# Two half pairs' weighted sums in one block every twelve steps, in an attention and expert kernel

## The chip, the core and the metric

One of the eight cores of a Trainium2 chip runs the kernel. The metric is the device time of one execution in microseconds (us). Engines: TensorE (PE; its weight loads are a queue of their own, PEld), VectorE (DVE), ScalarE (ACT), GpSimd (POOL) and SyncE (SP, which issues DMAs).

## The reference

Attention in which a query sees only the keys of its own hash bucket, and then a layer of eight experts with one expert per token:

```python
q_bits = (einsum('bhsd,dk->bhsk', q, proj) > 0)         # q, k, v: (4, 8, 768, 64); proj: (64, 6)
mask   = q_bucket[..., :, None] == k_bucket[..., None, :]
attn   = softmax(where(mask, scale * q @ k.T, -1e9))     # divided by (sum + 1e-9)
x      = (attn @ v).transpose(0, 2, 1, 3).reshape(3072, 512)
e_idx  = argmax(x @ w_gate)                              # 8 experts
out[t] = gate_w[t] * sigmoid(x[t] @ w_output_gate)[e] * (relu(x[t] @ w1[e]) @ w2[e])   # w1: 512x1024
```

## The kernel before

**The steps.** The 32 heads form 16 pairs. A pair has 2 heads x 6 query tiles of 128 rows, so 12 tiles, and the attention is a loop over 192 steps, one tile each. The order of instructions on PE, DVE, ACT and POOL is the order in which the code issues them; nothing reorders it. What one tile passes through:

- `scores`: four matmuls (L548) into `ps_s`, one of two PSUM buffers, then VectorE's eviction (L552), which clips, takes the row minimum and frees the buffer;
- `soft`: ScalarE's exponential in place (L560), which also sums each row;
- `normal`: for two tiles together, VectorE adds 1e-9 to the row sums and inverts them (L567, L568), and GpSimd scales the two tiles (L570);
- `transposed`: six TensorE transposes (L586) into the two buffers of `ps_t`, and two ScalarE copies from there into `pts` (L591);
- `weighted`: for a half pair (six tiles), 24 matmuls with the values into `ps_a` (L601), VectorE's copy into `ot` (L604), and in `rows` VectorE's transpose into `xb` (L613) and the DMA to `x_dram`.

Step s issues scores of tile s and, LAG = 6 steps behind, the transposes of tile s - 6. At every sixth step there is a **block** between these two: the weighted sums of one half pair, which need only data that is ready, and beneath them five exponentials on ScalarE (2 + 2 + 1). The sixth exponential of the six steps stands at the second step behind the block (k == 2), alone between the copies of two tiles. Two of the three pairs of tiles are scaled in the block, the third at k == 3.

**What else is hung into the steps.** `plan(step, fn)` puts work at the end of a step, `block(step, when, fn)` into a block at a named place. The projection of the next pair's queries and keys (`project`, 0.85 us of TensorE, and VectorE's sign bits, L417), the splitting of these into high and low parts (`split_hi` on GpSimd L495, `split_lo` on VectorE L502), and for each batch of four pairs the routing: `logits` and `tokens` (the experts' logits, transposed), `best` and `choose` (one-hot of the expert, ending in the cast L678 to `ohb`), `prefix` (matmuls of `ohb` with a triangle, L702, which give each token's place), `ranks`, `places` (L201 to L208), `gate_values` and `columns` (L689 to L218), `hot` (L223), and a table by matmuls (L229). Of the last batch but one, `pick` (L804 to L813) chooses an expert whose tokens and weights are then fetched and prepared (L178 to L181) while attention still runs.

Behind step 191 the remaining six tiles are transposed and copied alone (of the odd ones the transposes go to `ps_s`), then the expert stage follows, with the sums of the last half pair inside its first matmuls.

Of the kernel before, what the change touches and what calls it, by code (L numbers as in the profile page):

```python
# [59 lines left out]
def lsh_attention_then_moe(  # L60
# [61 lines left out]
    perm = cst.tile([P, E, E], F32, name="perm")  # L122
# [131 lines left out]
    def gather(idx, n=CH, ntok=NTOK, pool=gp, bufs=NCH):  # L254

        xg = pool.tile([CH, DM], F32, name="xg", bufs=bufs)
# [114 lines left out]
    with ExitStack() as actx:  # L371
# [14 lines left out]
        LAG = PER  # L386
# [153 lines left out]
        def scores(s):  # L540
# [10 lines left out]
            mn = sp.tile([P, 1], F32, name="mn", bufs=PER + 2)  # L551
# [20 lines left out]
        def transposed(s, pr):  # L572
# [6 lines left out]
            two = ps_s.tile([P, 2, 512], F32, name="ps_s") if last and s % 2 else None  # L579
            for h in range(2):  # L580
                if two is None:
                    tr = ps_t.tile([P, 3, P], F32, name="ps_t")
                else:
                    tr = two[:, h, 0:HS].rearrange("p (c q) -> p c q", c=3)
                for c in range(3):
                    nc.tensor.transpose(tr[:, c], pr[:, (3 * h + c) * P:(3 * h + c + 1) * P], ident)  # L586
                dst = pts[:, 3 * h:3 * h + 3, t * P:(t + 1) * P]
                if h and last:
                    nc.vector.tensor_copy(dst, tr)
                else:  # L590
                    nc.scalar.copy(dst, tr)  # L591

        def weighted(hb, c):
            g, hf = hb // 2, hb % 2
            st = pairs[g]
            if c == 0:
                st["av"] = ps_a.tile([P, HS], F32, name="ps_a")
            if c == NT - 1 and hf == 0:
                st["ot"] = gp.tile([P, S], F32, name="ot", bufs=4)
# [3 lines left out]
            if c == NT - 1:  # L603
                nc.vector.tensor_copy(st["ot"][:, hf * HS:(hf + 1) * HS], st["av"])  # L604
# [18 lines left out]
        def routing(b):  # L623
# [5 lines left out]
            def logits(hf, n):  # L629
                if hf == 0:  # L630
                    st["lt"] = gp.tile([P, S], F32, name="lt")
                pm = ps_m.tile([P, HS], F32, name="ps_m")
# [112 lines left out]
        for g in range(NP):  # L745
            s0 = 12 * (g - 1)
            if g >= 2:
                plan(max(s0 - 20, 8) if g > 2 else 2, lambda g=g: load(g))
                if g > 2:
                    block(s0 - PER, "matmuls", lambda g=g: project(g))  # L750
                else:
                    plan(8, lambda g=g: project(g))
                block(s0, "head", *(lambda g=g, j=j: split_hi(g, j) for j in range(2)))
                block(s0, "early", lambda g=g: split_lo(g, 0, 0))
                block(s0, "amid", lambda g=g: split_lo(g, 0, 1), lambda g=g: split_lo(g, 1, 0))
                block(s0, "behind", lambda g=g: split_lo(g, 1, 1), *(lambda g=g, j=j: spread(g, j) for j in range(2)))
            elif g == 1:
# [4 lines left out]
                for j in range(2):  # L762
                    for n in range(2):
                        plan(3 + n + (4 + n) * j, lambda j=j, n=n: split_lo(1, j, n))
                    plan(4 + 5 * j, lambda j=j: spread_lo(1, j), lambda j=j: spread_bits(1, j))
                plan(6, lambda: load_v(0))
            if g >= 1:
                plan(s0 + 10, lambda g=g: load_v(g))
            for hf in range(2 if g + 1 < NP else 1):
                block(12 * g + 6 * hf + 2 * PER, "matmuls", *(  # L770
                    lambda hb=2 * g + hf, c=c: weighted(hb, c) for c in range(NT)))
                if g + 1 < NP:
                    plan(12 * g + 6 * hf + 2 * PER, lambda g=g, hf=hf: rows(g, hf))
        for i, fn in enumerate(more_constants()):
            plan(18 + 2 * i, fn)
        for b in range(B - 1):
            r = routing(b)
            s0 = 12 * (H // 2) * (b + 1)
            for hf in range(2):
                block(s0 + PER * (hf + 1), "logits", lambda r=r, hf=hf: r["logits"](hf, H // 2))  # L780
            block(s0 + 3 * PER, "amid", r["choose"], r["gate_sums"])
            block(s0 + 5 * PER, "amid", r["gate_values"], r["columns"])
# [424 lines left out]
```

## Time and profile before

| | us |
|---|---|
| median of 3 runs (lowest, highest) | 760.28 (760.21, 760.89) |
| the profiled execution: its time, its span | 761.32, 759.6 |
| PE busy | 743.7 (98% of the span) |
| PEld busy | 606.1 (80%) |
| DVE busy | 489.6 (64%) |
| ACT busy | 459.9 (61%) |
| POOL busy | 377.2 (50%) |

The time of the profiled execution is longer than its span by 1.72 us, which lie around it. A share is an average over two stages: attention with routing up to about 440 us, the experts behind it. All rows of the trace below count from the start of the span.

### The profile page before, as it was taken

The page shows a single profiled execution, that of the slowest core. Times are in us where ns is not written, and L with a number is a line of the kernel's source. Part 1 is how long each engine was busy: PE and PEld are TensorE (multiplying, and loading weights), DVE is VectorE, ACT ScalarE, POOL GpSimd, SP SyncE. Part 2 cuts the span into 40 slices and gives each one's busy share as a digit, 9 for nine tenths or more (in the row PEclk, how much of TensorE's full clock was granted, in tenths as well). Part 3 has the DMA queues.
Part 4 walks back from the last instruction along what each step waited for, and adds up shares of the span by engine and source line. Part 5 has one row for each costly group of instructions (what it writes and reads, how often), then busy time and mean ns, then how long its engine had stood idle before and what let it go on. Part 6 is the DMA issues. An engine that isn't in the chain of part 4 may idle for free. (4 is left out here: it accounts for less than half of the span.)

```text
span 759.6 us, 13708 instructions
## 1 busy us (share of the span) xinstructions
PE 743.7 (98%) x4690; PEld 606.1 (80%) x4690; DVE 489.6 (64%) x1043; ACT 459.9 (61%) x930; POOL 377.2 (50%) x415
## 2 busy tenths in 40 slices
PE   7999999999999999999999999999999999999997
PEld 5776867677676777768687678888999999989895
DVE  7867776797776888667897684266353545454540
ACT  6778887877888787888888721253333344443331
POOL 6556553554555355454457923535446464645201
PEclk9999999999999999999999999999999999999999
DMA  6465555456565545555353422373434444536601
GB/s 208 117 151 133 121 134 124 109 126 136 128 124 125 127 106 130 131 133 120 77 118 108 122 59 84 103 270 118 131 128 152 160 151 155 184 123 223 203 12 40
DMA packets 84799, 98.89 MB, mean 130 GB/s; under 512 B 57999, under 2 KB 59439, under 8 KB 84720
## 3 DMA queue, kind: packets, MB, share of 16 engines
q1 hardware_dynamic: 79376, 84.58, 42.8%
q0 software_dynamic: 5200, 13.31, 5.4%
q8 instruction: 40, 0.66, 0.4%
q14 instruction: 39, 0.32, 0.1%
q10 hardware_dynamic: 144, 0.02, 0.0%
HBM read 59.49 MB, written 13.11 MB: 96 GB/s over the span
## 5 line engine op out<-in xcount | busy, mean ns | idle before, releaser
L570 POOL TENSOR_SCALAR sc<-sc,rsum 128x768 f32<-128x768 f32 x192 | 186.6, 985 | 188.4 <-DVE rsum L568 93.7
L552 DVE TENSOR_SCALAR_CACHE_REDUCE sc<-ps_s 128x768 f32<-128x768 f32 x192 | 182.4, 954 | 52.0 <-PE ps_s L548 47.8
L591 ACT COPY pts<-ps_t 128x384 f32<-128x384 f32 x375 | 161.4, 483 | 80.6 <-PE ps_t L586 79.8
L560 ACT ACTIVATE sc<-sc,mn 128x768 f32<-128x768 f32 x192 | 178.2, 935 | 4.0 <-DVE sc L552 4.0
L586 PE MATMUL ps_t<-ident,sc 128*128 128x128 f32 x1134 | 158.2, 275 | 0.0
L586 PEld LDWEIGHTS ps_t<-ident,sc 128*128 128x128 f32 x1134 | 132.0, 141 | 28.1 <-POOL sc L570 14.7
L601 PE MATMUL ps_a<-pts,vt 128*64 128x384 f32 x768 | 131.1, 490 | 0.0
L548 PE MATMUL ps_s<-xr,xl 128*128 128x384 f32 x384 | 114.7, 380 | 4.0 <-DVE sc L552 2.7
L601 PEld LDWEIGHTS ps_a<-pts,vt 128*64 128x64 f32 x768 | 52.2, 137 | 67.7 <-issue 67.5
L326 DVE SCALAR_TENSOR_TENSOR hl<-ps_s,hh 128x256 fp32r<-128x256 f32 (+8 forms) x40 | 34.0, 849 | 109.1 <-ACT hh L325 95.6
L548 PE MATMUL ps_s<-yr,yl 76*128 76x384 f32 x384 | 99.2, 339 | 1.0 <-POOL yr L455 1.0
L315 PE MATMUL ps_s<-xh,w1h 128*128 128x256 f32 (+7 forms) x288 | 97.0, 337 | 0.2 <-DVE hl L326 0.2
L315 PE MATMUL ps_s<-xh,w1l 128*128 128x256 f32 (+7 forms) x288 | 95.2, 331 | 0.3 <-DVE w1l L181 0.3
L315 PE MATMUL ps_s<-xlo,w1h 128*128 128x256 f32 (+7 forms) x288 | 95.3, 331 | 0.0
L289 POOL DMA_INDIRECT xq<-x_dram,idx x75 | 82.1, 1095 | 23.8 <-issue 20.8
L332 POOL DMA_INDIRECT out_dram<-yo,sid x29 | 30.9, 1067 | 120.6 <-ACT yo L331 76.4
L325 ACT ACTIVATE hh<-ps_s 128x256 fp32r<-128x256 f32 (+8 forms) x40 | 29.1, 727 | 101.5 <-PE ps_s L315 71.6
L548 PEld LDWEIGHTS ps_s<-yr,yl 76*128 76x128 f32 x384 | 70.1, 190 | 1.5 <-POOL yr L455 1.5
L548 PEld LDWEIGHTS ps_s<-xr,xl 128*128 128x128 f32 x384 | 58.3, 192 | 6.9 <-DVE sc L552 4.8
L315 PEld LDWEIGHTS ps_s<-xh,w1h 128*128 128x128 f32 x288 | 54.2, 188 | 2.5 <-DVE hl L326 0.7
L315 PEld LDWEIGHTS ps_s<-xh,w1l 128*128 128x128 f32 x288 | 54.1, 188 | 1.8 <-DVE w1l L181 0.7
L315 PEld LDWEIGHTS ps_s<-xlo,w1h 128*128 128x128 f32 x288 | 54.1, 188 | 1.3 <-DVE xlo L272 0.2
(211 smaller groups left out, 1021.1 us busy)
## 6 DMA issues: line engine op xcount, KB each, us to landing
w_raw<-in_w_dram SPq DMA_DIRECT2D x34, 512.0 KB
qk<-in_qkT_dram SPq DMA_DIRECT2D x32, 384.0 KB
xh<-in_w_dram SPq DMA_DIRECT2D x14, 512.0 KB
xlo<-in_w_dram SPq DMA_DIRECT2D x14, 512.0 KB
vt<-in_v_dram SPq DMA_DIRECT2D x16, 384.0 KB
xr<-xl SPq DMA_DIRECT2D x30, 192.0 KB
yr<-xl SPq DMA_DIRECT2D x30, 192.0 KB
xr<-yl SPq DMA_DIRECT2D x30, 192.0 KB
```

The source lines that it names most:

```text
L289: nc.gpsimd.indirect_dma_start(out=xq[:, k * P:(k + 1) * P], out_offset=None, in_=x_dram.rearrange("n (a f) -> (n a) f", a=NB32), in_offse ...
L315: nc.tensor.matmul(ps, l, r, start=first and k == 0, stop=last and k == len(pairs) - 1)
L325: nc.scalar.activation(hh, ph, AF.Relu)
L326: return lambda: nc.vector.scalar_tensor_tensor(hl, ph, 0.0, f32(hh), ALU.max, ALU.subtract)
L332: nc.gpsimd.indirect_dma_start(out=out[:, :], out_offset=bass.IndirectOffsetOnAxis(ap=sid[0:n, r, a:a + 1], axis=0), in_=yo[0:n], in_offse ...
L548: nc.tensor.matmul(ss[:, n, 0:HS], l[0:k, qs], r[0:k, n * HS:(n + 1) * HS], start=first, stop=not first)
L552: nc.vector.tensor_scalar(sc, ss[:, :, 0:HS], MASKED, None, ALU.min, ALU.min, accum_out=mn)
L560: nc.scalar.activation(pr, pr, AF.Exp, bias=mn, scale=-1.0, accum_out=sums[s // GROUP][:, k:k + 1])
L570: nc.gpsimd.tensor_scalar(live[s0 + k], live[s0 + k], rs[:, k:k + 1], 0.0, ALU.mult, ALU.add)
L586: nc.tensor.transpose(tr[:, c], pr[:, (3 * h + c) * P:(3 * h + c + 1) * P], ident)
L591: nc.scalar.copy(dst, tr)
L601: nc.tensor.matmul(st["av"][j * D:(j + 1) * D], st["v"][:, j, c], blocks[hb][j][:, c], start=(c == 0), stop=(c == NT - 1))
```

## The change

The block stands at every twelfth step, two steps later than before (SHIFT = 2: steps 14, 26, ... 194), and has the sums of two half pairs: the second half of one pair ("sums", into `ps_a`), then the first half of the next pair ("more", into `ps_m`). The transposes run LAG = 8 steps behind the scores (from step 14 on). Nine exponentials stand in the block (2 + 2 + 2 + 2 + 1), three alone at k = 2, 4 and 6. Four pairs of tiles are scaled in the block, the others at k = 3 and k = 7 (or k = 1). The copy of "more" out of `ps_m` ("done") stands behind routing work on VectorE. The logits go into `ps_t` and are copied by ScalarE behind the nine exponentials. `choose` moves out of a block to the end of a step with k = 7, one step ahead of `prefix`; `places` and `gate_values` with `columns` move into blocks. In the last six tiles, odd ones are copied by one ScalarE instruction. Two allocations move (`perm`, and the tiles of later gathers) and some loads, splits and weight preparations move by some steps.

```diff
-        LAG = PER
+        SHIFT = 2
+        LAG = PER + SHIFT
+        LONG = 2 * PER
...
-                dst = pts[:, 3 * h:3 * h + 3, t * P:(t + 1) * P]
-                if h and last:
-                    nc.vector.tensor_copy(dst, tr)
-                else:
-                    nc.scalar.copy(dst, tr)
+                    nc.tensor.transpose(trs[h][:, c], pr[:, (3 * h + c) * P:(3 * h + c + 1) * P], ident)
+                if two is None:
+                    (nc.vector.tensor_copy if h and last else nc.scalar.copy)(
+                        pts[:, 3 * h:3 * h + 3, t * P:(t + 1) * P], trs[h])
+            if two is not None:
+                nc.scalar.copy(pts.rearrange("p (h c) q -> p h c q", h=2)[:, :, :, t * P:(t + 1) * P],
+                               two[:, :, 0:HS].rearrange("p h (c q) -> p h c q", c=3))
...
-                st["av"] = ps_a.tile([P, HS], F32, name="ps_a")
+                st["av"] = (ps_a if hf else ps_m).tile([P, HS], F32, name="ps_a" if hf else "ps_m")
...
+        def weighed(hb):
+            g, hf = hb // 2, hb % 2
+            st = pairs[g]
+            if hf == 0:
+                st["ot"] = gp.tile([P, S], F32, name="ot", bufs=4)
+            nc.vector.tensor_copy(st["ot"][:, hf * HS:(hf + 1) * HS], st["av"])
...
-                pm = ps_m.tile([P, HS], F32, name="ps_m")
+                pm = ps_t.tile([P, HS], F32, name="ps_t")
...
+                at_block = LONG * ((hb + 3) // 2) + SHIFT
+                block(at_block, "sums" if hf else "more", *(lambda hb=hb, c=c: weighted(hb, c) for c in range(NT)))
+                block(at_block, "sums" if hf else "done", lambda hb=hb: weighed(hb))
+                if g + 1 < NP and hf:
+                    block(at_block, "routing", lambda g=g: rows(g, 1))
...
-            block(s0 + 3 * PER, "amid", r["choose"], r["gate_sums"])
-            block(s0 + 5 * PER, "amid", r["gate_values"], r["columns"])
...
+            block(s0 + LONG + SHIFT, "logits", *(lambda r=r, hf=hf: r["logits"](hf, H // 2) for hf in range(2)))
+            block(s0 + 2 * LONG + SHIFT, "routing", r["places"])
+            block(s0 + 3 * LONG + SHIFT, "routing", r["gate_values"], r["columns"])
+            for n, fn in ((15, lambda r=r: r["tokens"](0, H // 2)), (17, lambda r=r: r["tokens"](1, H // 2)),
+                          (19, r["best"]), (21, r["choose"]), (22, r["prefix"]), (23, r["gate_sums"]), (24, r["ranks"]),
+                          (42, r["hot"]), (44, r["table"]), (45, r["entries"])):
+                plan(s0 + n, fn)
...
-                    now("amid")
+                    now("project")
+                    normals()
                     softs(2)
+                    now("amid")
+                    normals()
+                    softs(2)
+                    now("behind")
                     normals()
-                    for when in ("logits", "matmuls", "behind"):
-                        now(when)
+                    softs(2)
+                    normals()
+                    now("sums")
+                    now("routing")
                     softs(1)
-                elif k == 3:
+                    for when in ("more", "logits", "done"):
+                        now(when)
+                elif k in (1, 3, 7):
                     normals()
-                if s >= LAG:
-                    transposed(s - LAG, live.pop(s - LAG))
-                if s >= PER and (k == 2 or s < 2 * PER and k in (1, 4)):
+                i = s - PER if s < LONG else s - LAG
+                if s >= PER and not LONG <= s < LONG + SHIFT:
+                    transposed(i, live.pop(i))
+                if s in (PER + 1, PER + 2, PER + 4) or s >= LONG + SHIFT and k in (2, 4, 6) or s >= NSTEP:
                     softs(1)
```

Line numbers of the changed kernel are a few higher from L548 on. Three places show how instructions stand. **ScalarE, two blocks of the second batch** (`L560`/`L561` is the exponential, `L591`/`L590` the copies of transposed tiles, x2 for the two halves of one). Before:

```order
L560 ACTIVATE sc,rsum<-sc,mn 128x768 x5
L591 COPY pts_2121<-ps_t 128x3x128 x2
L591 COPY pts_2122<-ps_t 128x3x128 x2
L591 COPY pts_2121<-ps_t 128x3x128 x2
L560 ACTIVATE sc,rsum<-sc,mn 128x768
L591 COPY pts_2122<-ps_t 128x3x128 x2
L591 COPY pts_2121<-ps_t 128x3x128 x2
L591 COPY pts_2122<-ps_t 128x3x128 x2
L560 ACTIVATE sc,rsum<-sc,mn 128x768 x5
```

The same engine in the changed kernel:

```order
L561 ACTIVATE sc,rsum<-sc,mn 128x768 x9
L590 COPY pts_2347<-ps_t 128x3x128 x2
L590 COPY pts_2348<-ps_t 128x3x128 x2
L590 COPY pts_2347<-ps_t 128x3x128 x2
L561 ACTIVATE sc,rsum<-sc,mn 128x768
L590 COPY pts_2348<-ps_t 128x3x128 x2
L590 COPY pts_2347<-ps_t 128x3x128 x2
L561 ACTIVATE sc,rsum<-sc,mn 128x768
L590 COPY pts_2348<-ps_t 128x3x128 x2
L590 COPY pts_2470<-ps_t 128x3x128 x2
L561 ACTIVATE sc,rsum<-sc,mn 128x768
```

Of twelve exponentials two stood alone between copies, now three do, with two tiles' copies between one and the next.

**VectorE at the choice of the expert** (`ohb` is what the prefix matmuls read; `sc,mn<-ps_s` is the eviction of scores). Before, in the block of step 66:

```order
L567 TENSOR_SCALAR rsum<-rsum 128x2
L568 RECIPROCAL rsum<-rsum 128x2
L671 TENSOR_SCALAR eq<-df 128x48
L672 TENSOR_TENSOR eq<-eq,expi 128x48
L674 TENSOR_REDUCE ei<-eq 128x6
L675 TENSOR_TENSOR oneh<-ei,expi 128x48
L678 CAST ohb<-oneh 128x48
L682 TENSOR_REDUCE den<-ex 128x6
L683 TENSOR_TENSOR en<-en,oneh 128x48
L685 TENSOR_REDUCE es<-en 128x6
```

Now at step 69, in the open steps, where TensorE has the scores and transposes of step 70 between this place and the prefix matmuls:

```order
L553 TENSOR_SCALAR sc,mn<-ps_s 128x768 x2
L568 TENSOR_SCALAR rsum<-rsum 128x2
L569 RECIPROCAL rsum<-rsum 128x2
L677 TENSOR_SCALAR eq<-df 128x48
L678 TENSOR_TENSOR eq<-eq,expi 128x48
L680 TENSOR_REDUCE ei<-eq 128x6
L681 TENSOR_TENSOR oneh<-ei,expi 128x48
L684 CAST ohb<-oneh 128x48
L553 TENSOR_SCALAR sc,mn<-ps_s 128x768 x2
```

The five instructions are the same; weighted sums ran beside them before, scores and transposes do now.

**VectorE at the gate values and columns** (`den` to `gate`, then `t_rhs`). Before, in the block of step 78, ahead of the second pair of row sums and of the copy out of `ps_a`:

```order
L567 TENSOR_SCALAR rsum<-rsum 128x2
L568 RECIPROCAL rsum<-rsum 128x2
L689 TENSOR_SCALAR den<-den 128x6
L690 TENSOR_SCALAR es<-es 128x6
L691 RECIPROCAL den<-den 128x6
L692 RECIPROCAL es<-es 128x6
L693 TENSOR_TENSOR gate<-den,es 128x6
L214 TENSOR_TENSOR t_rhs<-oneh,t_oa 128x192
L218 TENSOR_TENSOR t_rhs<-t_rhs,toki 128x192
L218 TENSOR_TENSOR t_rhs<-t_rhs,gate 128x192
L567 TENSOR_SCALAR rsum<-rsum 128x2
L568 RECIPROCAL rsum<-rsum 128x2
```

Now in the block of step 86, behind the fourth pair of row sums, the copy out of `ps_a` and its transpose:

```order
L619 STREAM_TRANSPOSE xb<-ot 128x384
L695 TENSOR_SCALAR den<-den 128x6
L696 TENSOR_SCALAR es<-es 128x6
L697 RECIPROCAL den<-den 128x6
L698 RECIPROCAL es<-es 128x6
L699 TENSOR_TENSOR gate<-den,es 128x6
L213 TENSOR_TENSOR t_rhs<-oneh,t_oa 128x192
L217 TENSOR_TENSOR t_rhs<-t_rhs,toki 128x192
L217 TENSOR_TENSOR t_rhs<-t_rhs,gate 128x192
L610 COPY ot<-ps_m 128x384
L553 TENSOR_SCALAR sc,mn<-ps_s 128x768 x3
```

The copy out of `ps_m` and the first eviction behind the block stand behind these eight instructions.

## Rows read from the trace of the kernel before

**Rows 1.** The profile page, the costliest groups of instructions over the whole program: line, engine, operation, out<-in, count | busy us, mean ns of one | idle time before them and what ended most of it.

```profile
L570 POOL TENSOR_SCALAR sc<-sc,rsum 128x768 f32<-128x768 f32 x192 | 186.6, 985 | 188.4 <-DVE rsum L568 93.7
```

**Rows 2.** Busy time of each engine in the stretch from the first weighted sum to the last transpose (us, then per engine busy time and count of instructions; the last three columns are the granted clock of TensorE as a share, the DMA share and GB/s).

```profile
29.60:441.50 411.90, 407.84 (x2843) 302.23 (x2842) 315.24 (x789) 328.06 (x749) 229.08 (x259) 1.00 0.54 124
```

**Rows 3.** The timeline of one block of before without routing work in it (start us, us, engine, line, operation, out<-in, count [idle before <-releaser]; a row of several instructions lasts from the first to the last of them): TensorE, then VectorE.

```profile
200.00 0.51 PE L548 MATMUL ps_s<-yr,yl 76*128 76x384 f32 x2
200.35 0.82 PE L586 MATMUL ps_t<-ident,sc 128*128 128x128 f32 x6
200.93 0.60 PE L548 MATMUL ps_s<-xr,xl 128*128 128x384 f32 x2
201.36 0.51 PE L548 MATMUL ps_s<-yr,yl 76*128 76x384 f32 x2
201.80 4.09 PE L601 MATMUL ps_a<-pts,vt 128*64 128x384 f32 x24
...
206.60 0.88 PE L586 MATMUL ps_t<-ident,sc 128*128 128x128 f32 x6
207.24 0.59 PE L548 MATMUL ps_s<-xr,xl 128*128 128x384 f32 x2
...
203.61 0.17 DVE L567 TENSOR_SCALAR rsum<-rsum 128x2 f32<-128x2 f32 x1 [0.64 <-ACT sc L560]
205.45 0.54 DVE L567 TENSOR_SCALAR rsum<-rsum 128x2 f32<-128x2 f32 x1 [1.47 <-ACT sc L560]
206.11 0.54 DVE L604 COPY ot<-ps_a 128x384 f32<-128x384 f32 x1
207.34 0.57 DVE L613 STREAM_TRANSPOSE xb<-ot 128x384 f32<-128x384 f32 x1
208.33 0.96 DVE L552 TENSOR_SCALAR_CACHE_REDUCE sc<-ps_s 128x768 f32<-128x768 f32 x1 [0.42 <-PE ps_s L548]
```

**Rows 4.** The timeline from the second to the fourth step behind that block, where one exponential stands between the copies of two tiles: ScalarE and TensorE, then the row sum that follows.

```profile
210.67 0.95 ACT L560 ACTIVATE sc<-sc,mn 128x768 f32<-128x768 f32 x1
211.76 0.51 PE L548 MATMUL ps_s<-yr,yl 76*128 76x384 f32 x2
212.22 0.85 PE L586 MATMUL ps_t<-ident,sc 128*128 128x128 f32 x6
212.82 0.60 PE L548 MATMUL ps_s<-xr,xl 128*128 128x384 f32 x2
...
211.93 0.16 DVE L567 TENSOR_SCALAR rsum<-rsum 128x2 f32<-128x2 f32 x1
```

**Rows 5.** The waits of TensorE's weight loads over the whole program (waiting engine and line <- what ended the wait: us in total, times, longest).

```profile
PEld ps_t L586 <- POOL sc L570: 14.7, 24, 0.6
PEld ps_t L586 <- issue: 7.4, 22, 0.6
```

**Rows 6.** The timeline around the block of step 66, whose second half pair of exponentials has the choice of the expert among them: VectorE's first and last instruction of the choice, then TensorE up to the prefix sums.

```profile
150.16 0.17 DVE L567 TENSOR_SCALAR rsum<-rsum 128x2 f32<-128x2 f32 x1 [0.65 <-ACT sc L560]
151.72 0.84 DVE L678 CAST ohb<-oneh 128x48 bf16<-128x48 f32 x1
...
153.16 0.88 PE L586 MATMUL ps_t<-ident,sc 128*128 128x128 f32 x6
154.38 0.18 PE L702 MATMUL ps_m<-ohb,tri 128*128 128x48 bf16 x1 [0.34 <-DVE bt L417]
```

**Rows 7.** The timeline of VectorE's routing work: the places of one batch (four steps after its prefix sums; the second row is the first instruction behind them), then the gate values and columns in the block of step 78 (first instruction, and the first one behind them).

```profile
160.87 0.32 DVE L201 TENSOR_TENSOR t_ge<-rank,chki 128x30 f32<-128x30 f32 x1
162.86 0.94 DVE L552 TENSOR_SCALAR_CACHE_REDUCE sc<-ps_s 128x768 f32<-128x768 f32 x1
...
177.00 0.15 DVE L689 TENSOR_SCALAR den<-den 128x6 f32<-128x6 f32 x1
179.63 0.15 DVE L567 TENSOR_SCALAR rsum<-rsum 128x2 f32<-128x2 f32 x1
```

**Rows 8.** The timeline of a late eviction behind the block of step 72 (the scores, the eviction of the step before, the weight loads that waited), and the first and last row of the pick of the leading expert (its first instruction, and the first one behind it).

```profile
167.44 0.52 PE L548 MATMUL ps_s<-yr,yl 76*128 76x384 f32 x2
168.95 0.92 DVE L552 TENSOR_SCALAR_CACHE_REDUCE sc<-ps_s 128x768 f32<-128x768 f32 x1
169.93 0.30 PEld L548 LDWEIGHTS ps_s<-xr,xl 128*128 128x128 f32 x2 [0.20 <-DVE sc L552]
...
384.25 0.16 DVE L804 SCALAR_TENSOR_TENSOR o_key<-base,expi 128x8 f32<-128x8 f32 x1
385.44 0.95 DVE L552 TENSOR_SCALAR_CACHE_REDUCE sc<-ps_s 128x768 f32<-128x768 f32 x1
```

**Rows 9.** The timeline of one GpSimd instruction of the expert stage's preparation (an expert's weights being split) and of ScalarE's copy of the logits out of PSUM.

```profile
430.14 2.37 POOL L181 TENSOR_TENSOR w1l<-w_raw,w1h 128x1024 fp32r<-128x1024 f32 x1
432.79 0.46 ACT L637 COPY lt<-ps_m 96x384 f32<-96x384 f32 x1
```

**Rows 10.** TensorE in the third step behind the first block of the program: the wait for an eviction.

```profile
38.58 0.61 PE L548 MATMUL ps_s<-xr,xl 128*128 128x384 f32 x2 [1.32 <-DVE sc L552]
```

**Rows 11.** TensorE over the last six tiles: the first transposes, one of the waits, the first instruction of the expert stage.

```profile
433.38 0.88 PE L586 MATMUL ps_t<-ident,sc 128*128 128x128 f32 x6
435.15 0.55 PE L586 MATMUL ps_s<-ident,sc 128*128 128x128 f32 x3 [0.57 <-ACT pts L591]
439.90 0.36 PE L315 MATMUL ps_s<-xh,w1h 128*128 128x256 f32 x1
```

More of the change, by code (lines that the diff above doesn't have):

```diff
@@ L550, in scores @@
             sc = tp.tile([P, 2, HS], F32, name="sc", bufs=LAG + 2)
-            mn = sp.tile([P, 1], F32, name="mn", bufs=PER + 2)
+            mn = sp.tile([P, 1], F32, name="mn", bufs=LAG + 2)
             nc.vector.tensor_scalar(sc, ss[:, :, 0:HS], MASKED, None, ALU.min, ALU.min, accum_out=mn)
@@ L749, in lsh_attention_then_moe @@
                 if g > 2:
-                    block(s0 - PER, "matmuls", lambda g=g: project(g))
+                    block(s0 + SHIFT, "project", lambda g=g: project(g))
                 else:
                     plan(8, lambda g=g: project(g))
[L753 to L756, printed above, removed]
+                block(s0 + SHIFT, "head", *(lambda g=g, j=j: split_hi(g, j) for j in range(2)))
+                block(s0 + SHIFT, "early", lambda g=g: split_lo(g, 0, 0))
+                block(s0 + SHIFT, "amid", lambda g=g: split_lo(g, 0, 1), lambda g=g: spread(g, 0),
+                      lambda g=g: split_lo(g, 1, 0))
+                block(s0 + SHIFT, "behind", lambda g=g: split_lo(g, 1, 1), lambda g=g: spread(g, 1))
             elif g == 1:
@@ L778, in lsh_attention_then_moe @@
             s0 = 12 * (H // 2) * (b + 1)
-            for hf in range(2):
-                block(s0 + PER * (hf + 1), "logits", lambda r=r, hf=hf: r["logits"](hf, H // 2))
-            block(s0 + 3 * PER, "amid", r["choose"], r["gate_sums"])
-            block(s0 + 5 * PER, "amid", r["gate_values"], r["columns"])
-            for n, fn in ((8, lambda r=r: r["tokens"](0, H // 2)), (14, lambda r=r: r["tokens"](1, H // 2)),
-                          (15, r["best"]), (18, r["prefix"]), (20, r["ranks"]), (22, r["places"]),
-                          (31, r["hot"]), (33, r["table"]), (34, r["entries"])):
-                plan(12 * (H // 2) * (b + 1) + n, fn)
+            block(s0 + LONG + SHIFT, "logits", *(lambda r=r, hf=hf: r["logits"](hf, H // 2) for hf in range(2)))
[5 more added lines that the diff above has]
+                plan(s0 + n, fn)
         r = routing(B - 1)
@@ L791, in lsh_attention_then_moe @@
         for hf in range(2):
-            block(s0 + PER * (hf + 1), "logits", lambda hf=hf: r["logits"](hf, lp))
-            plan(s0 + PER * (hf + 1) + 2, lambda hf=hf: r["tokens"](hf, lp))
+            block(s0 + LONG + SHIFT, "logits", lambda hf=hf: r["logits"](hf, lp))
+            plan(s0 + LONG + SHIFT + 2 * hf + 1, lambda hf=hf: r["tokens"](hf, lp))
         late = 12 * (H // 2) * (B - 1) + 26
@@ L859, in early_gather @@
             gid = lead_slots(0)
-            early["xg"] = [gather(gid[:, a:a + 1], CH, NTOK - S) for a in range(EARLY)]
+            early["xg"] = [gather(gid[:, a:a + 1], CH, NTOK - S, gp, EARLY) for a in range(EARLY)]
         def early_turn(a):
@@ L1003, in lsh_attention_then_moe @@
     mp = ctx.enter_context(tc.tile_pool(name="mp", bufs=1, reuse_waits="tile"))
+    perm = mp.tile([P, E, E], F32, name="perm")
     with tc.manual_schedule(engines=MANUAL):
```

50 lines of the change are left out of this document (24 added, 26 removed).

## The prediction

> **What bounds the kernel now.** I read the page first: TensorE is busy for 98% of the span, GpSimd for half, and its scalings take 0.99 us each [rows 1]. Then busy time by stretch: between the first sums and the last transposes TensorE is busy for 407.84 of 411.90 us, at a granted clock of 1.00 [rows 2]. So attention is bound by TensorE's instructions in their written order, and a change of order can win back only idle time (4.06 us there) and slow steps. Then the timeline, for the price of a step: scores of two neighbouring steps are 1.36 us apart (200.00 and 201.36) [rows 3], and the reader is to see that nothing else fits between them. All times below stand in the frame of this block, whose sums begin at 201.80.
>
> **1. Fewer entries and exits.** Ahead of the sums the gap from scores to the next instruction is 0.44 us (201.36 to 201.80), in an open step 0.35 (200.00 to 200.35); behind them transposes take 0.64 (206.60 to 207.24) instead of 0.58 (200.35 to 200.93) [rows 3]. A block thus costs 0.15 beside its work. The weight loads show the exits: 24 waits of 0.6, and some of the 22 in the row beneath [rows 5]. Before had 31 blocks in the loop (steps 12 to 192 by 6), now there are 16 (14 to 194 by 12): 15 x 0.15 = **-2.2**. A measured sum, which I take without bounds.
>
> **2. More exponentials in the open.** An exponential of 0.95 stands between two tiles' copies; transposes two steps later start 0.46 behind their scores instead of 0.35, and take 0.60 instead of 0.58 [rows 3, 4]: their PSUM buffer comes free late. Price 0.13. The 22 waits sum to 7.4 us [rows 5]; with exits of 0.6 and lone exponentials of 0.23 that is 6 and 16, so 16 of the 31 lone ones of before cost, 2.1 us; the others lie beside table, token or late steps. Three per twelve steps over 15 cycles are 45. In the rows ScalarE has caught up two steps later, so each pays anew; I let 39 pay (six beside tokens): 5.1 - 2.1 = **+3.0**. Bounds: as many absorbed as before (23 x 0.13 = 3.0), +0.9; all 45 at 0.16, +5.1.
>
> The Trainium skill, "Perfetto Trace Analysis", section Identifying Performance Opportunities, says that a gap repeating on the engine that should be saturated can mean too few buffers; the trace agrees, since the change triples what waits for two `ps_t` buffers, and by that all 45 pay, which is the upper bound.
>
> **3. The choice ahead of the prefix sums.** Before, from the row sum at 150.16 to the cast's end at 152.56 took 2.40 us, under weighted sums; the prefix matmul was still held until 154.38, 0.58 behind the end of transposes begun at 153.16 (+0.64), three times 1.7 [rows 6]. Now `choose` starts behind row sums at k = 7, where GpSimd begins to scale as well. By the like of it in the open steps: row sum at 211.93, prefix matmuls wanted at 212.82, when the second transposes from there are through [rows 4]; 211.93 + 2.40 = 214.33, a wait of 1.5, three times: 4.5 - 1.7 = **+2.8**. Lower bound: the cast at 0.17 instead of 0.84, as a small instruction takes without GpSimd beside it (203.61 against 205.45, 0.17 and 0.54) [rows 3], and one more like it: 1.0 less per choice, -0.2. Upper: 0.2 more each, +3.4. What queues behind: only an eviction that has a step's room. I take the middle chain, since GpSimd scales two tiles through all of it.
>
> **4. Routing ahead of the copy from `ps_m`.** This decides. VectorE executes in order: fourth row sums, copy from `ps_a`, transpose, routing, copy from `ps_m`, first eviction behind the block. Two exponentials are 1.84 apart in row sums (203.61, 205.45), so the fourth pair's stands at 209.13. With 0.66 for it (205.45 to 206.11), 0.54 for the copy and 0.57 for the transpose, VectorE reaches routing at 210.90. Second sums add 4.02 (4.09 from first to last end, less the overlap), so the eviction is wanted at 208.33 + 4.02 = 212.35 [rows 3]. An eviction may be 0.65 late: at 168.95 it was 0.85 behind its place (1.09 behind the scores' first half, that is 0.66 behind the second at 167.44), and TensorE waited 0.20 [rows 8]. So routing and its 0.54 copy must end by 213.00: routing may take 1.55.
> Places took 1.99 (160.87 to 162.86), gate values and columns 2.63 (177.00 to 179.63) [rows 7], both partly beside GpSimd. Alone I estimate 0.95 and 1.45, with contended instructions at 0.2 instead of 0.6 to 0.9. GpSimd's fourth pair, two scalings of 0.99 [rows 1], starts at about 209.8 and ends near 211.8, or near 212.7 with earlier pairs delayed, so I take the middle: places 1.75, a wait of 0.2 (two blocks); columns 2.25, a wait of 0.7 (two blocks); the block of step 170, where `pick` (1.19, 384.25 to 385.44) [rows 8] follows places: 0.2 + 1.1 = 1.3; the block of step 182, with a weight split of 2.37 [rows 9] ahead of the scalings, 1.6. Sum 0.4 + 1.4 + 1.3 + 1.6 = 4.7, less four late evictions of before of 0.2 or less (the first in [rows 8]), 0.7: **+4.0**. Bounds: uncontended, 0.9 in all (pick and the split alone), +0.2; the full measured chains, 0.45, 1.1, 1.6 and 2.4, 7.1 - 0.7 = +6.4. In plain blocks VectorE is in time: 210.90 + 0.54 is ahead of 212.35.
>
> In this place a row shows the mechanism: the same two-element row sum takes 0.17 alone and 0.54 beside a scaling [rows 3]. The Trainium skill, "SBUF — State Buffer", section Reading the diagram, says that GpSimd and a VectorE instruction with two SBUF inputs, or a copy or cast in its fast mode, take a shared port pair as an exclusive lock for the whole instruction. It speaks against moving these instructions behind eight scalings; what follows from full blocking is rival D.
>
> **5. Logits in `ps_t`.** ScalarE's copy out takes 0.46 [rows 9]. The second logits end as late as the sums allow, and the second half of the next transposes needs that buffer: about 0.3 in four blocks, **+1.2** (0, if the copy of the first is enough; 1.4).
>
> **6. Start.** Behind the first block TensorE waited 1.32 for an eviction [rows 10], since splits and row sums stood ahead of it on VectorE. They stand there in step 14 too; before it, steps 12 and 13 have scores without transposes and outrun evictions of 0.96 [rows 3] by about 0.5: **+0.5** (-1.3 if the wait goes, +1).
>
> **7. Tail.** The last six tiles take 6.52 us (433.38 to 439.90) with waits such as 0.57 for ScalarE's copy [rows 11]; 36 transposes at 0.58 for six are 3.5, so about 2.9 are waits. Now the last exponentials lie under sums, one ScalarE instruction empties an odd tile, but tokens and token turns come among them: **-0.9** (-2 to 0).
>
> Loads, `perm`, later gathers: nothing, hidden by 50% idle GpSimd and DMA share 0.54 [rows 2]; `hot` (0.95 on VectorE) in an open step costs up to 0.35 each where it delays an eviction beyond 0.65; I take 0.
>
> Sum: -2.2 + 3.0 + 2.8 + 4.0 + 1.2 + 0.5 - 0.9 = **+8.4**. On the profiled 761.3 that is 769.7, on the median 760.28, 1.0 lower, **768.7**. All lower ends: -2.2 + 0.9 - 0.2 + 0.2 + 0 - 1.3 - 2 = -4.6, 755.7; all upper ends: +15.1, 775.4.
>
> **The rivals.**
> - A, the forecast: 768.7, itself 766.5 to 772.
> - B, GpSimd is done when routing begins: term 4 at its lower end, total +4.6, 764.9. For it: the fourth scaling may end at 211.8, 0.9 into routing. Against: the four splits of the block contend before it.
> - C, VectorE is in time everywhere (the other side): with twelve steps' cover under one block, routing that made TensorE wait in open steps no longer does. Prefix waits (-1.7), late evictions (-0.7), the start (-1.3) vanish, logits cost nothing; with -2.2, +3.0 and -0.9: -3.8, 756.5. It decides where routing in a block stays within 1.55 and a choice within 0.9. For it: TensorE is hardly stopped now; against: 2.40, 1.99 and 2.63 in rows.
> - D, each routing piece meets two whole scalings (0.95 + 1.8 and 1.45 + 1.8): waits 0.65, 1.65, 1.8 and 2.4, 8.8 - 0.7 = +8.1 in term 4, total +12.5, 772.8. For it: GpSimd's pairs may end at 212.7; against: no row here shows two in succession lost to one piece.
> - E, gains and costs cancel, since lone exponentials are hidden as often as before and B holds: -2.2 + 0.9 + 2.8 + 0.2 + 0.6 - 0.9 = +1.4, 761.7, about the same.
>
> **How the numbers follow.** The three runs of before spread by 0.09%, so 0.2% (1.5 us) is about what can be told from no change. Chances: A 0.46, B 0.15, C 0.17, D 0.13, E 0.09. The range 757 to 773.5 leaves out a lower half of C and an upper half of D. Faster 0.17 (C), same 0.09 (E, with edges of B), slower 0.74.
>
> **What would show it.** Term 1: fewer waits of 0.6 for transposes. Term 2: three waits of about 0.24 per twelve steps. Term 3: prefix matmuls waiting for `ohb` by 1.5. Term 4: scores waiting for an eviction behind the blocks of steps 74, 86, 122, 134, 170 and 182, and not behind plain ones. Term 5: the first transposes behind four blocks. I am wrong if evictions behind routing blocks start within 0.65 of their place, or if ScalarE's copies keep up behind lone exponentials.

## The result, and the profile after

The changed kernel takes 771.35 us (median of four runs, 768.71 to 772.66), the kernel before 760.25 on the same chips: a ratio of 1.0138, 95% interval 1.0125 to 1.015, so slower by 1.4%. Forecast were 768.7 and a range of 757 to 773.5. The profiled execution took 770.70 with a span of 768.6, 9.0 more than before. The first matmul of the experts starts at 449.75 after the start of the span and 443.06 after the first scores; before, 439.90 [rows 11] and 433.14. So attention lost 9.9 us, and the rest of the program gave 0.8 back.

The page after, the stretch of [rows 2] again, and the waits of TensorE that answer to [rows 5] (waiting engine and line <- what ended the wait: us in total, times, longest), with one such row of before at their end:

```profile
PE 743.9 (97%) x4690; PEld 609.6 (79%) x4690; DVE 501.4 (65%) x1040; ACT 461.5 (60%) x930; POOL 376.7 (49%) x415
```

```profile
29.60:441.50 411.90, 399.52 (x2771) 298.19 (x2772) 322.00 (x778) 324.13 (x739) 223.52 (x255) 1.00 0.51 119
```

```profile
PEld ps_s L549 <- DVE sc L553: 12.1, 11, 2.6
PEld ps_t L588 <- issue: 10.1, 36, 0.6
PEld ps_t L588 <- POOL sc L571: 7.6, 12, 0.7
PE ps_m L708 <- DVE ohb L684: 3.9, 3, 1.3
...
PEld ps_s L548 <- DVE sc L552: 4.8, 7, 1.6
```

TensorE has as much work as before (743.9 us), but in the same stretch is idle for 12.4 us instead of 4.1. The exits that waited 0.6 for transposes have become fewer (24 to 12), waits of the weight loads on evictions of scores have grown from 4.8 to 12.1 us, and the prefix sums wait three times for `ohb`.

The best view of the loss is the distance from the first scores of a step to those of the next, since TensorE sets it. A plain step is 1.36 in both. What differs, worked out from the starts of all 192 steps (us):

| | before | after | difference |
|---|---|---|---|
| blocks, beyond a step, their sums at 4.02, projection and logits at 0.78 | 30 x 0.15 | 0.2 | -4.3 |
| steps lengthened by a lone exponential (1.49, or 2.83 with a table) | 15 x 0.13 | 29 x 0.13 | +1.8 |
| the prefix step, three times | 0.77 beyond its block | 1.86 beyond a step | +3.3 |
| late evictions behind routing | 0.8 | 0.6, 0.6, 0.9, 0.9, 1.6, 2.7 | +6.6 |
| steps 185 and 186 at a lower clock | | 1.5 | +1.5 |
| logits blocks (12.00 instead of 11.74) | | 3 x 0.26 | +0.8 |
| start (steps 12, 13 and 16 against step 14) | 1.6 | 2.0 | +0.4 |
| end: turns and tokens gone from the loop, longer from step 191 to the experts | | | -0.1 |

The sum is +10.0, the 9.9 but for rounding.

**Choice and prefix sums.** The timeline of the changed kernel at step 69 (VectorE, GpSimd, TensorE), which answers to [rows 6]:

```profile
152.52 0.16 DVE L568 TENSOR_SCALAR rsum<-rsum 128x2 f32<-128x2 f32 x1
153.07 1.79 POOL L571 TENSOR_SCALAR sc<-sc,rsum 128x768 f32<-128x768 f32 x2 [4.11 <-ACT pts L590]
153.48 0.55 DVE L681 TENSOR_TENSOR oneh<-ei,expi 128x48 f32<-128x48 f32 x1
154.07 0.83 DVE L684 CAST ohb<-oneh 128x48 bf16<-128x48 f32 x1
154.96 0.18 PE L708 MATMUL ps_m<-ohb,tri 128*128 128x48 bf16 x1 [1.31 <-DVE ohb L684]
```

From the row sum to the cast's end are 2.38 us, of which the last 1.8 lie beside two scalings, and TensorE stands for 1.31. Only the one-hot and the cast are longer than 0.21 us, and they end about when the first and the second scaling do.

**Places** in the block of step 74 (the two rows of `t_ge` and `t_pos` are the first and the last of them), against [rows 7]:

```profile
163.24 8.04 POOL L571 TENSOR_SCALAR sc<-sc,rsum 128x768 f32<-128x768 f32 x8 [6.50 <-DVE rsum L569]
168.96 0.58 DVE L200 TENSOR_TENSOR t_ge<-rank,chki 128x30 f32<-128x30 f32 x1
169.58 0.85 DVE L203 TENSOR_TENSOR t_oa<-t_ge 128x24 f32<-128x24 f32 x1
170.54 0.74 DVE L207 SCALAR_TENSOR_TENSOR t_pos<-t_na,rank 128x6 f32<-128x6 f32 x1
171.21 0.55 DVE L610 COPY ot<-ps_m 128x384 f32<-128x384 f32 x1
```

Places take 2.25 us, from 168.96 to 171.21. Three of their four instructions are long; they end at 169.54, 170.43 and 171.28, each within 0.04 us of the end of a scaling. The reduction between them took 0.16.

**Gate values and columns** in the block of step 86:

```profile
195.29 0.58 DVE L695 TENSOR_SCALAR den<-den 128x6 f32<-128x6 f32 x1
197.31 0.35 DVE L217 TENSOR_TENSOR t_rhs<-t_rhs,gate 128x192 f32<-128x192 f32 x1
197.58 0.55 DVE L610 COPY ot<-ps_m 128x384 f32<-128x384 f32 x1
198.05 0.95 DVE L553 TENSOR_SCALAR_CACHE_REDUCE sc<-ps_s 128x768 f32<-128x768 f32 x1
199.06 0.30 PEld L549 LDWEIGHTS ps_s<-xr,xl 128*128 128x128 f32 x2 [0.93 <-DVE sc L553]
```

Routing takes 2.29 us ahead of the copy from `ps_m`, the eviction comes at 198.05 and the scores two steps on wait 0.93.

**The block of step 182**, GpSimd, VectorE and TensorE:

```profile
413.33 0.51 DVE L695 TENSOR_SCALAR den<-den 128x6 f32<-128x6 f32 x1
415.73 1.14 POOL L177 TENSOR_SCALAR w1h<-w_raw 128x1024 fp32r<-128x1024 f32 x1
415.88 1.19 DVE L217 TENSOR_TENSOR t_rhs<-t_rhs,gate 128x192 f32<-128x192 f32 x1
416.99 0.55 DVE L610 COPY ot<-ps_m 128x384 f32<-128x384 f32 x1
418.47 0.50 PEld L549 LDWEIGHTS ps_s<-xr,xl 128*128 128x128 f32 x2 [2.65 <-DVE sc L553]
419.92 1.48 PE L588 MATMUL ps_t<-ident,sc 128*128 128x128 f32 x6
```

and busy time by stretch around it (columns as in [rows 2]):

```profile
416.00:418.40 2.40, 0.06 (x1) 0.00 (x0) 2.40 (x5) 0.63 (x2) 2.32 (x2) 0.95 0.47 71
418.40:420.00 1.60, 1.53 (x5) 1.44 (x6) 0.89 (x4) 1.03 (x2) 0.91 (x1) 0.50 0.00 0
420.00:421.00 1.00, 1.00 (x7) 1.00 (x6) 0.75 (x1) 0.20 (x1) 0.00 (x0) 0.50 0.65 115
422.00:426.00 4.00, 4.00 (x32) 3.68 (x31) 3.63 (x7) 3.07 (x8) 3.92 (x4) 1.00 0.07 27
```

The weight loads stand for 2.65 us and the matmuls for 2.41, and then six transposes take 1.48 instead of 0.82: the granted clock is 0.50 for some 3 us, which is the lower of the two levels, 1.2 GHz.

### The profile page after: what moved, and what is told of

It is laid out like the page before. It is cut to its first block, busy times and chain, and to the rows that moved or that the text cites. A ratio compares the mean times of both kernels' runs of the same rounds, so it can differ in the third digit from the quotient of the medians.

```text
span 768.6 us, 13762 instructions
## 1 busy us (share of the span) xinstructions
PE 743.9 (97%) x4690; PEld 609.6 (79%) x4690; DVE 501.4 (65%) x1040; ACT 461.5 (60%) x930; POOL 376.7 (49%) x415
## 5 line engine op out<-in xcount | busy, mean ns | idle before, releaser
L590 ACT COPY pts<-ps_t 128x384 f32<-128x384 f32 x375 | 161.8, 484 | 79.6 <-PE ps_t L588 79.5
L561 ACT ACTIVATE sc<-sc,mn 128x768 f32<-128x768 f32 x192 | 178.3, 936 | 6.7 <-DVE sc L553 6.5
L549 PEld LDWEIGHTS ps_s<-xr,xl 128*128 128x128 f32 x384 | 58.8, 193 | 14.1 <-DVE sc L553 12.1
L602 PE MATMUL ps_a<-pts,vt 128*64 128x384 f32 x384 | 65.7, 491 | 0.0
L602 PE MATMUL ps_m<-pts,vt 128*64 128x384 f32 x384 | 64.7, 486 | 0.0
L602 PEld LDWEIGHTS ps_a<-pts,vt 128*64 128x64 f32 x384 | 26.1, 137 | 37.0 <-issue 36.8
```

The costliest lines, as they stand in the source:

```text
L549: nc.tensor.matmul(ss[:, n, 0:HS], l[0:k, qs], r[0:k, n * HS:(n + 1) * HS], start=first, stop=not first)
L561: nc.scalar.activation(pr, pr, AF.Exp, bias=mn, scale=-1.0, accum_out=sums[s // GROUP][:, k:k + 1])
L590: (nc.vector.tensor_copy if h and last else nc.scalar.copy)(pts[:, 3 * h:3 * h + 3, t * P:(t + 1) * P], trs[h])
L602: nc.tensor.matmul(st["av"][j * D:(j + 1) * D], st["v"][:, j, c], blocks[hb][j][:, c], start=(c == 0), stop=(c == NT - 1))
```

## The experiments

All are edits of the changed kernel, each executed once except the last two; single steps are compared, and the distance from the first scores to the experts' first matmul (443.06 after, 433.14 before). Steps that an edit leaves alone repeat to 0.01 us where the clock stays up, those behind a block with routing to about 0.2; the first twelve steps, ahead of every edit, took 22.0 us before and after, and 20.7 to 22.5 in these runs.

**Is it VectorE's order, and does something queue behind the choice?** The choice one step earlier:

```diff
-                          (19, r["best"]), (21, r["choose"]), (22, r["prefix"]), (23, r["gate_sums"]), (24, r["ranks"]),
+                          (19, r["best"]), (20, r["choose"]), (22, r["prefix"]), (23, r["gate_sums"]), (24, r["ranks"]),
```

> The changed kernel with the choice of the expert issued one step earlier (k = 6 instead of 7), so that VectorE runs it ahead of the row sums and GpSimd's scaling, not beside them. Theory (order and contention): the cast takes 0.2 instead of 0.83 and the one-hot 0.2 instead of 0.55, the choice about 1.3 us; the wait of 1.31 us of the prefix matmuls goes at all three places, the next eviction comes about 0.9 late, 0.25 more than its room, and the lone exponential of that step costs its 0.13 again: about -0.8 us at each of three, some -2.4 us in all. Rival (the choice takes 2.4 us wherever it stands): the prefix wait goes, but an eviction is 2 us late and holds the scores two steps later by 1.35 us: no gain in all.

764.3 us, 438.10 to the experts. The choice takes 1.13 us, ahead of the scaling:

```profile
151.13 0.18 DVE L677 TENSOR_SCALAR eq<-df 128x48 f32<-128x48 f32 x1
152.07 0.19 DVE L684 CAST ohb<-oneh 128x48 bf16<-128x48 f32 x1
153.61 0.19 PE L708 MATMUL ps_m<-ohb,tri 128*128 128x48 bf16 x1
```

The cast is 0.19, not 0.83, and the prefix matmuls wait for nothing. Their step falls from 3.21 to 1.75; a later step, 73, rises to 1.85, and step 76, behind the places, falls from 1.92 to 1.36, which neither side expected (last section). Net -1.4 at two places and -1.2 at the third. Steps 185 and 186 give another 1.5, since the clock stayed up in this run, and small losses elsewhere take 0.5 back: 5.0 gained.

**The same wait, moved on instead of removed.** The prefix matmuls one step later:

```diff
-                          (19, r["best"]), (21, r["choose"]), (22, r["prefix"]), (23, r["gate_sums"]), (24, r["ranks"]),
+                          (19, r["best"]), (21, r["choose"]), (23, r["prefix"]), (23, r["gate_sums"]), (24, r["ranks"]),
```

> The changed kernel with the prefix matmuls (and the gate sums) one step later, the choice where it is, beside GpSimd's scaling. As the prediction had it (behind the choice queues only an eviction that has a step's room): the wait of 1.31 us goes and nothing takes its place, -1.2 us at each of three places, -3.6 us in all. Rival (VectorE's lateness is the cost, whoever waits): the eviction behind the choice started 1.8 us behind its place, 1.15 more than the 0.65 of room that the trace of before shows, so the scores two steps on wait 1.1 to 1.2 us instead: less than 0.2 us gained at each.

769.2 us. The 1.31 us wait is gone, and in its place step 71 takes 2.41, waiting for an eviction:

```profile
155.52 0.62 PE L549 MATMUL ps_s<-xr,xl 128*128 128x384 f32 x2 [0.53 <-DVE sc L553]
```

That is 0.79 more than a step with these matmuls takes where nothing waits (1.62: the 1.75 of the run before, less 0.13 for a lone exponential). Steps 70 and 71 together go from 4.57 to 3.90, a gain of 0.7, where 1.2 (nothing queues) or less than 0.2 was expected. So neither figure holds; that lateness passes to the eviction does.

**What do GpSimd's scalings cost VectorE?** No scaling beside choice and routing:

```diff
             nc.vector.reciprocal(rs, rs)
+            if s in (69, 117, 165, 74, 86, 122, 134, 170, 182):
+                return
             for k in range(GROUP):
```

> The changed kernel without GpSimd's scalings in steps 69, 117 and 165 and in the blocks of steps 74, 86, 122, 134, 170 and 182 (these tiles stay unscaled, which this run leaves out of the computation); all other instructions and their order stay. Theory (contention with GpSimd lengthens the routing chains): the choice takes 1.4 instead of 2.3 us, the prefix wait falls from 1.31 to about 0.4; places take 0.95 instead of 2.25 and columns 1.5 instead of 2.3, and the waits behind those blocks (0.32 and 0.69 on TensorE) go, that of step 172 (1.38) falls to about 0.3; that of step 184 (2.41) falls only in part, since the weight split on GpSimd stays. In all about -6 us. Rival (VectorE's chain is as long without GpSimd, order alone is the cause): the waits stay within 0.2 us of what they are.

760.7 us, 434.25 to the experts: -8.8, of which 1.5 is the clock that stayed up. The steps behind the blocks of 74, 86, 122, 134 and 170 are plain again, that of 182 takes 2.26 instead of 4.02. Places in the block of step 74 take 0.57 us, 168.80 to 169.37, where they took 2.25:

```profile
168.80 0.15 DVE L200 TENSOR_TENSOR t_ge<-rank,chki 128x30 f32<-128x30 f32 x1
168.98 0.18 DVE L203 TENSOR_TENSOR t_oa<-t_ge 128x24 f32<-128x24 f32 x1
169.37 0.55 DVE L612 COPY ot<-ps_m 128x384 f32<-128x384 f32 x1
```

Only the choice kept most of its wait, 0.90:

```profile
153.05 0.91 POOL L496 TENSOR_SCALAR xl<-qk,pj 128x768 fp32r<-128x768 f32 x1 [3.65 <-PE ps_s L549]
153.24 0.76 DVE L679 TENSOR_SCALAR eq<-df 128x48 f32<-128x48 f32 x1
154.99 0.18 PE L710 MATMUL ps_m<-ohb,tri 128*128 128x48 bf16 x1 [0.90 <-DVE ohb L686]
```

GpSimd, free of the scaling, had begun the next split of keys instead, and the first small instruction took 0.76 beside that. So contention with GpSimd, whatever it runs, makes nearly all of term 4. In the block of step 182 0.90 is left:

```profile
404.54 2.38 POOL L180 TENSOR_TENSOR w1l<-w_raw,w1h 128x1024 fp32r<-128x1024 f32 x1
411.38 0.62 PE L549 MATMUL ps_s<-xr,xl 128*128 128x384 f32 x2 [0.65 <-DVE sc L553]
```

Routing itself ran from 408.42 to 409.90, behind the split and with GpSimd idle. The split had held up the row sums ahead of it (one took 2.23 us), and this block has no projection, since no pair follows: its step takes 9.40 instead of 10.18, so VectorE has 0.78 us less under it.

**Lone exponentials.** 64 columns instead of 768:

```diff
...
-                    softs(1)
+                    softs(1, 64 if LONG + SHIFT <= s < NSTEP else 2 * HS)
```

> The changed kernel with the three lone exponentials per twelve steps (k = 2, 4, 6) over 64 columns instead of 768, so 0.25 instead of 0.93 us of ScalarE each (scalings multiply by a tiny constant so that numbers stay finite; the rest of these tiles is left out). Theory (a lone exponential makes the copies late and the transposes two steps later wait for their PSUM buffer): the 26 steps of 1.49 us become 1.36, the table steps lose 0.13 too: -3.9 us, steps elsewhere unchanged. Rival (the two tile copies of a step and the buffers are short of each other anyway): the steps stay at 1.49.

All 26 steps of 1.49 are 1.36, the table steps 2.70, as the theory had it: 3.8 us in all. To the experts only 1.6 is gained (441.45), since steps 88, 136, 172 and 184 came out 0.1 to 0.2 longer and the lower clock took 2.9 us instead of 1.5. (The tokens' experts differ without these numbers, so the expert stage of this run, and its total of 885, can't be compared.)

**Routing out of the blocks:**

```diff
-            block(s0 + 2 * LONG + SHIFT, "routing", r["places"])
-            block(s0 + 3 * LONG + SHIFT, "routing", r["gate_values"], r["columns"])
...
+                          (25, r["places"]), (35, r["gate_values"]), (36, r["columns"]),
...
-        plan(late, pick)
+        plan(late + 2, pick)
```

> The changed kernel with places, gate values and columns out of the blocks: places at the last open step ahead of the block (s0 + 25), gate values and columns at steps s0 + 35 and 36, the pick two steps behind its block; the choice stays. Theory (routing between the fourth row sums and the copy from ps_m makes evictions late, and GpSimd lengthens it): the steps behind the blocks of 74, 86, 122, 134, 170 and 182 fall to 1.36, two times 0.59, two times 0.95, 1.6 and 2.65 us less, and no fall of the clock behind the last one, 1.2; lone exponentials there cost their 0.13 again; in the open steps at most 0.2 us each of new waits. About -7.5 us to the first matmul of the experts (449.7 before it). Rival (VectorE has too much to do in the open steps as well): the waits come back there, more than half of the gain.

769.2 us, 440.76 to the experts: -2.3, not -7.5, and 1.3 of that lies in the first twelve steps, so -1.0. Behind all six blocks the waits are gone. Columns brought 0.6 back in steps 85 and 133, and in the last batch steps 181 and 182 took 3.69 and 12.56: a wait of 2.3, and then 3.2 over a block of 9.4, with a granted clock of 0.50 from 404 to 408. VectorE and GpSimd there:

```profile
403.23 2.37 POOL L180 TENSOR_TENSOR w1l<-w_raw,w1h 128x1024 fp32r<-128x1024 f32 x1
403.38 2.43 DVE L217 TENSOR_TENSOR t_rhs<-t_rhs,toki 128x192 f32<-128x192 f32 x1
```

An instruction of 0.36 us lasted as long as the weight split beside it. Places were cured; for the last batch the rival won.

**The weight split behind the scalings:**

```diff
-            plan(late + (7, 11, 14, 17)[cc], lambda cc=cc: early_w1(cc))
+            plan(late + (7, 13, 14, 17)[cc], lambda cc=cc: early_w1(cc))
```

> The changed kernel with one weight split of the early expert (GpSimd, 1.1 and 2.4 us) issued at step 183 instead of 181, so behind the scalings of the block of step 182 and not ahead of them. Theory (the split delays the scalings and lies beside the columns): the step 184, 4.01 us, falls to that of steps 88 and 136, about 2.4, with no fall of the clock: -1.6 us, or -2.9 where the clock fell. Rival (columns alone make it late): 4.0 as before.

772.6 us: step 184 took 5.67, longer than the 4.02 of the changed kernel. Both expectations missed:

```profile
415.13 1.21 POOL L177 TENSOR_SCALAR w1h<-w_raw 128x1024 fp32r<-128x1024 f32 x1
416.43 2.34 POOL L180 TENSOR_TENSOR w1l<-w_raw,w1h 128x1024 fp32r<-128x1024 f32 x1
416.47 2.51 DVE L217 TENSOR_TENSOR t_rhs<-t_rhs,gate 128x192 f32<-128x192 f32 x1
```

GpSimd begins a queued split as soon as the scalings ahead of it are through, here at 415.13, in the middle of the columns, though the code issues it a step later.

**Everything spread** over open steps without scalings:

```diff
...
+                          (19, r["best"]), (20, r["choose"]), (22, r["prefix"]), (24, r["ranks"]), (31, r["gate_sums"]), (32, r["gate_values"]),
+                          (36, r["places"]), (42, r["hot"]), (44, r["columns"]), (45, r["table"]), (46, r["entries"])):
...
-                    plan(at_block + 9, lambda g=g: rows(g, 0))
+                    plan(at_block + 2, lambda g=g: rows(g, 0))
...
+        plan(late + 2, pick)
...
```

> The changed kernel with all routing on VectorE spread over open steps in which GpSimd scales nothing: choice at s0 + 20, ranks 24, gate sums 31, gate values 32, places 36, hot 42, columns 44, table 45, entries 46; the transpose of the even half pair two steps behind the block instead of nine, the pick two steps behind its block. Theory (all of terms 3 and 4 is VectorE's lateness): no wait over 0.2 us behind blocks or ahead of prefix sums; of the 9.8 us to the experts' first matmul about 9.5 go, and since the saved 0.3 us per twelve steps stays, the time comes to 758.5 to 760.5, level with before. Rival (a long block with nine exponentials costs more than the shorter cycle saves, whatever routing does): 762 or more.

766.06 (764.39 to 766.92), ratio 1.0084, interval 1.007 to 1.0098. Two batches have no wait over 0.2 left; in the last, columns met the splits again (2.40 beside 2.35), and steps 189 and 190 took 6.88 and 2.15. That alone is 5 us. The total lies where the rival put it (762 or more), but not for the rival's reason: the theory had overlooked the splits.

**The last batch mended as well,** its VectorE work ahead of step 182 and all splits behind:

```diff
...
+            tail = ((25, r["places"]), (30, r["gate_sums"]), (32, r["gate_values"]), (35, r["columns"]), (37, r["hot"]),
+                    (44, r["table"]), (45, r["entries"])) if b == B - 2 else (
...
+            plan(late + (13, 14, 19, 22)[cc], lambda cc=cc: early_w1(cc))
+            plan(late + (3, 4, 16, 18)[cc], lambda cc=cc: early_load(cc))
...
```

> The spread version (e8) with the last routed batch mended: its places, gate sums, gate values, columns and hot at s0 + 25, 30, 32, 35 and 37, so ahead of step 182, and all four weight splits of the early expert issued behind the scalings of that block (steps 183, 184, 189, 192), since GpSimd starts a queued split as soon as its scalings are through, whatever step issues it; tables of the other batches one step later. Theory (a VectorE instruction with two SBUF operands waits for a whole split of 2.4 us): the waits of steps 189 and 190 of e8 (5.3 us beyond the table) go, 0.9 us of new ones in steps 172 to 181 at most; from the first scores to the experts' first matmul 432 us (433.1 before the change, 436.4 in e8), and 757 to 759 us in all, so 0.1 to 0.4% faster than the kernel before. Rival (the lateness moves to scalings and to the last block, which the splits now hold up): 761 or more.

759.81 (11 runs) against 761.08 of the kernel before (15 runs): ratio 0.9982, interval 0.9973 to 0.9991, a little faster than before the change, by the expected 0.1 to 0.4%, though the time is just above the expected 757 to 759; 431.55 to the experts. No step of routing waits:

```profile
394.45 0.35 DVE L213 TENSOR_TENSOR t_rhs<-oneh,t_oa 128x192 f32<-128x192 f32 x1
394.83 0.36 DVE L217 TENSOR_TENSOR t_rhs<-t_rhs,toki 128x192 f32<-128x192 f32 x1
395.11 0.35 DVE L217 TENSOR_TENSOR t_rhs<-t_rhs,gate 128x192 f32<-128x192 f32 x1
407.74 1.06 POOL L177 TENSOR_SCALAR w1h<-w_raw 128x1024 fp32r<-128x1024 f32 x1
```

The three instructions take 1.0 us where GpSimd is idle. All that made the changed kernel slower than before thus lay in where routing and splits stand, not in the long block itself.

## Why the prediction came out as it did

The direction and the range held, and 771.35 lies in the band of the likeliest case A (766.5 to 772), though nearer to the 772.8 of D than to the 768.7 of A. Term by term:

- **Term 1** (-2.2): measured -4.3. The entry and the exit beside a plain step were read rightly, and one pair of them is saved per twelve steps. What the step left out is that sums next to other sums are shorter. Starts in the changed block of step 110 (TensorE; 62 is the same):

```profile
239.21 0.85 PE L415 MATMUL ps_m<-qk,pjc 128*32 128x384 f32 x8
239.99 4.09 PE L602 MATMUL ps_a<-pts,vt 128*64 128x384 f32 x24
243.91 4.04 PE L602 MATMUL ps_m<-pts,vt 128*64 128x384 f32 x24
247.88 1.50 PE L641 MATMUL ps_t<-ot,wgt 128*32 128x384 f32 x16
```

  From start to start 3.92 and 3.97, where every block of before takes 4.02: another 0.15 per block. Of this 0.10 lies at the seam: the second sums start 0.32 behind the last matmul of the first, where a projection or transposes start 0.42 behind it. "A measured sum, which I take without bounds" was the mistake; no row of before has sums next to sums.
- **Term 2** (+3.0): +1.8. The price of 0.13 is exact (1.49 against 1.36, and the short exponentials take it away). The count was not: 29 pay, not 39, since ScalarE catches up wherever TensorE stands for another reason, behind routing, tokens and tables. The upper bound, that all 45 pay, which was also the reading of the Trainium skill's sentence on repeating gaps, was too high. That the copies free the two buffers late is shown by the short exponentials; no run here has more buffers, and lone exponentials went from two to three in twelve, so they did not triple.
- **Term 3** (+2.8): +3.3. The analogue with row sum, choice and scaling in the open steps gave 1.5; measured are 1.31 idle and 1.46 by the step (3.21 against 1.75 with the choice moved). The 0.58 of before was no wait for the choice, whose cast had ended at 152.56: [rows 6] names `bt`, the sign bits, as what ended it. "Only an eviction that has a step's room" was wrong: with the prefix moved, that eviction cost 0.79.
- **Term 4** (+4.0): +6.6, the lateness at the predicted steps and nowhere else, but larger at each. Places took 2.25 (1.75 forecast) and cost 0.56 instead of 0.2. Columns took 2.29 (2.25) but began 0.24 later against TensorE than reckoned, and cost 0.93 instead of 0.7. The block of step 170 cost 1.63 for 1.3. The evictions' room of 0.65 held. The block of step 182, 2.66 for 1.6, was mis-sized most, for two things that the sum lacked: it has no projection, so the first exponential stands 0.18 ahead of the sums (404.39, 404.57) and not 0.95 (185.93, 186.88 in the block of step 86); and a split already queued on GpSimd ran beside the last of the columns (1.19 instead of 0.35). The other split, which the text put ahead of the scalings, was there too. The run without scalings shows the cause that was argued. The Trainium skill, "SBUF — State Buffer", section Reading the diagram, was weighed there: an exclusive lock held for the whole instruction. The trace with routing out of the blocks agrees closely (0.36 became 2.43 beside a split of 2.37). Rival D, which took it in full with +8.1 for this term, came nearer to 6.6 than A did.
- **The clock** (+1.5) stood in no term.
- **Term 5** (+1.2): 0.26 in three blocks and 0.3 in the last, +1.1. **Term 6** (+0.5): +0.4. **Term 7** (-0.9): the stretch behind step 191 is longer by 1.4 than its extra sums, logits and transposes explain, and the turns and tokens that left the loop give 1.5 back, so -0.1 (-0.4 without the 0.3 that term 5 has). Two tiles' transposes stand alone there, 1.18 apart instead of 0.58, held by ScalarE's copies:

```profile
431.51 0.85 PE L588 MATMUL ps_t<-ident,sc 128*128 128x128 f32 x6 [0.33 <-ACT pts L590]
432.69 0.84 PE L588 MATMUL ps_t<-ident,sc 128*128 128x128 f32 x6 [0.33 <-ACT pts L590]
```

That the total is near is in part luck: term 1 was too small by 2.1, and term 4 with the clock too small by 4.1, the other way. Rival C, VectorE in time everywhere, is what the last experiment built by another order, at 0.2% faster.

## What to carry to other kernels

Where one engine is the bound, lay the two kernels side by side by the distance between its like steps: every wait shows as a step that is too long, and a price read once can be counted. Small VectorE instructions (here those with two tensors or a scalar, and the cast; not reductions or reciprocals, which kept their 0.2 us) can last, beside a long GpSimd instruction, until that one ends, so they belong where GpSimd is idle; and a GpSimd instruction runs when its queue reaches it, not in the step that issues it. A saving in one place (here 4.3 us from merged blocks) is only kept if the work that the merge displaces finds room elsewhere.

## What the runs showed that was not expected

- After a wait of some 2 us TensorE came back at half clock in some executions and not in others: behind 2.41 us in the changed kernel (0.50 from 418.4 to 421), behind 2.38 with the prefix moved and behind 2.09 with routing out of the blocks, but not behind 2.39 us with the choice moved (granted 1.00 throughout). It cost 1.5 us in the profiled execution. Runs of the changed kernel spread over 4 us, those of the kernel before over 1.1; that the clock is the reason is likely, since the slower an execution was, the lower was its mean granted clock (0.999, 0.994, 0.993 and 0.991 from 768.71 to 772.66), but it was not shown.
- Weighted sums took 4.02 us from start to start ahead of a projection, logits or transposes and 3.92 ahead of other sums, with the same 24 matmuls and whether scores, transposes or a projection stood ahead of them; those behind other sums took 3.97 instead of 4.02. What makes the difference stays open.
- With the choice one step earlier, the wait behind the places (0.56) went too, though the places took as long (0.57, 0.84, 0.74 beside scalings). In that run TensorE waited 0.49 in step 73, just ahead of the block, and ScalarE did not: its first exponential stood 1.49 us ahead of the sums (158.58, 160.07) instead of 0.96 (159.92, 160.88), so the fourth row sum, and all behind it, came 0.5 earlier against TensorE. The chain that ends in the late eviction begins with eight exponentials on ScalarE, which the prediction had only used as a starting time.
